# Seven block products in place of eight in the second layer, with stored sums of the weights

## The chip, the cores and the metric

The kernel runs on one core of one Trainium2 chip. The core has five engines that work side by side, each through its own instructions in order: TensorE (matrix products, PE in the profile, with PEld for the load of the operand that stays in the array), VectorE (DVE), ScalarE (ACT), GpSimd (POOL) and SyncE (SP), which here only issues DMA transfers. TensorE writes to the accumulators (PSUM), the other data live in SBUF, and DMA moves data between SBUF and the chip's memory. The metric is the device time of one execution in microseconds, the median of several runs.

## The reference, cut to what matters

The reference is an attention with a local window and block summaries, followed by two dense layers with a squared relu between them. There are 4 x 768 = 3072 tokens, 512 columns and 2048 inner columns.

```python
    k_sum = k.reshape(B, H, nb, block, D).max(axis=3)
    v_sum = v.reshape(B, H, nb, block, D).mean(axis=3)
...
    a = np.exp(scores_all)
    a = a / (np.sum(a, axis=-1, keepdims=True) + 1e-09)
    v_all = np.concatenate([v, v_sum], axis=2)
    return np.matmul(a, v_all).astype(np.float32)
...
    h = np.maximum(x @ w_in, 0.0)
    return (h * h @ w_out).astype(np.float32)
```

## The kernel before, in words

**Tiles, chunks and slots.** The 3072 tokens are 24 tiles of 128 (six for each of the four batches) and 12 chunks of two tiles (`CT` = 256 tokens). The 2048 inner columns are 16 units of 128 (`NF`). A slot does two units of one chunk, so a chunk is eight slots, numbered 0 to 7 in this document. Each operand of a product in the two layers is held as a high and a low part in a 32-bit format (float32r), and a product is made as high x high, high x low and low x high: three passes. The split weights of both layers stay in SBUF for the whole kernel, one tile `w_sb` per unit (first 512 columns for the first layer, the other 512 for the second).

**A slot** (`slot`) issues in this order: the first layer for both units (`ffn1`, L345: 2 x 12 products of 256 columns, into two accumulators `ph`), then the second layer of the slot before (`finish`, `ffn2`, L386: 2 units x 2 tiles x 3 passes = 12 products of 512 columns into `o_ps`), then for each unit the side steps of the attention that fall due and the squares (`squares`): relu on ScalarE (L354), square as the high part `gh` on ScalarE (L361), exact square on VectorE, written back over `ph` (L366), and the low part `gl` on VectorE (L370). The last step of a chunk is `evict`: ScalarE copies the two accumulators, SyncE stores them.

**The attention of later tiles** runs as twelve steps (`steps`), two per slot, one before each unit's squares (`side`) or at the slot's end (`last`). Two tiles are begun in every eight slots. From the fourth chunk on, this puts into the slots of a chunk:

- slots 0 and 4: steps 6 and 7, four transposes on VectorE (`turn`, L301) before the first unit's squares and four before the second's; for the first two tiles of a batch `place_v` stands with the second four.
- slots 1 and 5: step 8, the last four transposes before the first unit; at the slot's end `outputs` (L314) of that tile and `scores` (L238) of the next one on TensorE, with the loads of `v`, `q`, `k` and, for some tiles, the next batch's keys and values.
- slots 2 and 6: `split_x` of the finished tile and the softmax of three heads before the first unit, three more heads before the second. A head is a masked maximum on VectorE (L265) and an exponential on ScalarE (L273).
- slots 3 and 7: the inverse of the sums on VectorE (L282, L283), `norm` on POOL (L288), the last two heads and, for some tiles, `sum_k` before the first unit; the other inverse and `norm` and, for the same tiles, `sum_v` (L165, L168) before the second.

Nothing reorders this: each engine takes its instructions in the order of the program. Chunks 0 and 1 and the first seven tiles follow an order written out by hand (`START`), in which the weights are loaded and split as well.

Of the kernel before, what the change touches and what calls it, by code (L numbers as in the profile page):

```python
# [24 lines left out]
P = 128  # L25
# [5 lines left out]
NC4 = DM // P  # L31
SPARE = 1
# [38 lines left out]
def attn_ffn_kernel(ctx: ExitStack, tc: tile.TileContext, q, k, kt, v, vt, v0, w, masks, ident, mean, out):  # L71
# [6 lines left out]
    ps_s = ctx.enter_context(tc.tile_pool(name="ps_s", bufs=1, space=bass.MemoryType.PSUM))  # L78
    ps_x = ctx.enter_context(tc.tile_pool(name="ps_x", bufs=1, space=bass.MemoryType.PSUM))
    ps_h = ctx.enter_context(tc.tile_pool(name="ps_h", bufs=3, space=bass.MemoryType.PSUM))  # L80
    ps_o = ctx.enter_context(tc.tile_pool(name="ps_o", bufs=2, space=bass.MemoryType.PSUM))
# [8 lines left out]
    k_sb = [const.tile([P, 5, 2, NPAIR, NB], F32, name=f"k_sb{i}") for i in range(2)]  # L90
# [3 lines left out]
    q_sb = [const.tile([P, 2, NPAIR, 64], F32, name=f"q_sb{i}") for i in range(2)]  # L94

    e_sb = const.tile([P, H, P], F32, name="e_sb")
    pT = [const.tile([P, H, P], F32, name=f"pT{i}") for i in range(2)]
# [9 lines left out]


    def load_q(g):
        nc.sync.dma_start(out=q_sb[g % 2], in_=q[g // NT, g % NT])  # L110

    def load_k(g):
        nc.sync.dma_start(out=k_sb[g % 2][:, 0:4], in_=k[g // NT, g % NT])
# [8 lines left out]
    def sum_v0(vn):  # L122


        ps = ps_o.tile([P, DM], F32, name="o_ps")
# [44 lines left out]
    def place_k(g):  # L170
        nc.vector.tensor_copy(out=k_sb[g % 2][:, 4], in_=ksum.unsqueeze(1).to_broadcast([P, 2, NPAIR, NB]))
# [58 lines left out]
    def scores(g, p0, p1):  # L230


        if g not in s_ps:
            s_ps[g] = ps_s.tile([P, 2, NPAIR, P], F32, name="s_ps")
        for p in range(p0, p1):
            for r, s in ((0, 0), (1, 1), (0, 1), (1, 0)):
                rs, ss = slice(r * 64, r * 64 + 64), slice(s * 64, s * 64 + 64)
                nc.tensor.matmul(  # L238
                    s_ps[g][ss, r, p, 0:NK], lhsT=q_sb[g % 2][rs, s, p, :], rhs=k_sb[g % 2][rs, :, s, p, :],
# [3 lines left out]
    def scores_kt(g, p0, p1):  # L243

        if g not in s_ps:
            s_ps[g] = ps_s.tile([P, 2, NPAIR, P], F32, name="s_ps")
        for p in range(p0, p1):
            for k0, k1 in ((0, 96), (96, NK)):
                for r, s in ((0, 0), (1, 1), (0, 1), (1, 0)):
# [4 lines left out]
                        s_ps[g][ss, r, p, k0:k1], lhsT=q_sb[g % 2][rs, s, p, :], rhs=keys, start=True, stop=True  # L254
# [35 lines left out]
    def turn_pe(g, half):  # L290

        tp = ps_h.tile([P, 4, P], F32, name="ph")
# [4 lines left out]
    def turn(g, n0, n1):  # L297

        blocks = [(i, j) for i in range(4) for j in ((0, 1, 3) if i % 2 == 0 else (1, 2, 3))]
        for i, j in blocks[n0:n1]:  # L300
            nc.vector.transpose(  # L301
                out=pT[g % 2][j * 32 : j * 32 + 32, :, i * 32 : i * 32 + 32],
# [5 lines left out]
    def outputs(g):  # L308
        x_ps[g] = xp = ps_x.tile([P, NPAIR, P], F32, name="x_ps")

        for s in range(2):
            for h in range(H):
# [4 lines left out]
                    rhs=pT[g % 2][:, h, s * 64 : s * 64 + 64],  # L317
# [22 lines left out]
    def ffn1(c, f):  # L340
# [64 lines left out]

    n_g = B * NT
    n_c = n_g // TPC
    behind = []  # L410

# [239 lines left out]
```

## Time and profile before

| | us |
|---|---|
| median of three runs | 627.61 (626.56 to 628.18) |
| the profiled execution | 625.83 |
| its span, first to last instruction | 624.0 |
| PE busy in the span | 600.9 |
| DVE busy | 406.6 |
| ACT busy | 298.4 |
| POOL busy | 96.3 |

The span is the part of the profiled execution that the profile covers. Matrix products overlap in the pipeline, so the busy time and the mean of one product say less than the distance between starts: twelve products of 512 columns follow each other in 2.75 us, although each is shown as 391 ns long. In the lines of a profile, "out<-in" gives the written and the read tensors, "x" the count, and "[... <-X]" the idle time of the engine before the instruction with what ended it. A line number such as L345 is that of the kernel.

### The profile page before, as it was taken

To read this page: it belongs to the slowest core of one execution; us is meant where nothing else is said; L and a number is where in the kernel's file an instruction comes from. 1 tells how busy PE (TensorE), PEld (TensorE's weight loads), DVE (VectorE), ACT (ScalarE), POOL (GpSimd) and SP (SyncE) were. 2 spreads that over 40 slices of the span, in tenths; PEclk is the share of its full clock that TensorE was granted. 3 is DMA by queue.
4 is the path that set the end of the run, shared out by engine and by line. 5 is a ranking of instruction groups with operands and counts; after the bars stand their busy time and mean duration, and the time that the engine had idled before them with its cause. 6 is when DMAs were issued, how large, how long until landed. Compare 5 with 4: busy or idle time off the path is not lost.

```text
span 624.0 us, 13376 instructions
## 1 busy us (share of the span) xinstructions
PE 600.9 (96%) x5216; PEld 538.4 (86%) x5216; DVE 406.6 (65%) x1232; ACT 298.4 (48%) x855; POOL 96.3 (15%) x83
## 2 busy tenths in 40 slices
PE   3699999999999999999999999999999999999997
PEld 2598888988989988998988989899889989889996
DVE  4789789768766857757658668567566566563222
ACT  3788987333544353443534444434525525433322
POOL 2555762001210100101201101101101001010000
PEclk9979999999999999999999999999999999999999
DMA  9999510462032231320231321311201300000000
GB/s 308 388 339 334 203 51 18 154 199 104 26 121 68 85 119 48 106 68 35 68 112 43 119 83 71 119 47 51 75 24 46 103 1 26 35 2 1 35 0 35
DMA packets 19855, 60.38 MB, mean 97 GB/s; under 512 B 2768, under 2 KB 2896, under 8 KB 17744
## 3 DMA queue, kind: packets, MB, share of 16 engines
q1 hardware_dynamic: 19792, 59.53, 28.3%
q8 instruction: 41, 0.67, 0.5%
q14 instruction: 22, 0.18, 0.1%
HBM read 53.23 MB, written 6.29 MB: 95 GB/s over the span
## 4 chain that ended last, share of the span: by engine, by line
PE 92%; DVE 3%; DMA 2%; ACT 2%; SPq 0%; issue 0%; POOL 0%; DVEq 0%; POOLq 0%
PE ph L345 42%; PE o_ps L386 41%; PE x_ps L314 4%; PE s_ps L238 3%; DMA q_sb<-in_q 1%; DMA mask_sb<-in_masks 1%; DVE w_sb L224 1%; PE s_ps L253 1%; PE ph L294 1%; ACT e_sb L273 0%; PE o_ps L129 0%; ACT w_sb L106 0%; ACT w_raw L209 0%; SPq L152 0%; DVE sm L282 0%
## 5 line engine op out<-in xcount | busy, mean ns | idle before, releaser
L345 PE MATMUL ph<-xh,w_sb 128*128 128x256 f32 x1536 | 272.8, 280 | 0.9 <-DVE w_sb L224 0.7
L345 PEld LDWEIGHTS ph<-xh,w_sb 128*128 128x128 f32 x1536 | 238.5, 189 | 10.7 <-issue 2.9
L386 PE MATMUL o_ps<-w_sb,gh 128*128 128x512 f32 x768 | 238.0, 391 | 0.0
L345 PE MATMUL ph<-xl,w_sb 128*128 128x256 f32 x768 | 213.5, 278 | 0.2 <-DVE xl L331 0.2
L386 PEld LDWEIGHTS o_ps<-w_sb,gh 128*128 128x128 f32 x768 | 137.1, 188 | 24.9 <-issue 0.2
L386 PE MATMUL o_ps<-w_sb,gl 128*128 128x512 f32 x384 | 151.4, 394 | 0.9 <-DVE gl L370 0.9
L366 DVE TENSOR_TENSOR ph<-ph,r 128x256 f32<-128x256 f32 x192 | 82.5, 430 | 101.1 <-ACT r L354 98.6
L354 ACT ACTIVATE r<-ph 128x256 f32<-128x256 f32 x180 | 67.9, 377 | 167.0 <-PE ph L345 165.9
L345 PEld LDWEIGHTS ph<-xl,w_sb 128*128 128x128 f32 x768 | 145.1, 189 | 0.4 <-DVE xl L331 0.4
L288 POOL TENSOR_TENSOR e_sb<-e_sb,sm 128x480 f32<-128x480 f32 x43 | 43.4, 1010 | 402.7 <-DVE nmx L265 356.7
L273 ACT ACTIVATE e_sb<-e_sb,nmx 128x120 f32<-128x120 f32 x192 | 73.8, 386 | 66.3 <-DVE nmx L265 66.1
L301 DVE STREAM_TRANSPOSE pT<-e_sb 32x256 f32<-32x256 f32 x216 | 94.2, 436 | 5.2 <-POOL e_sb L288 1.8
L370 DVE TENSOR_TENSOR gl<-ph,gh 128x256 fp32r<-128x256 f32 x192 | 81.5, 424 | 24.3 <-ACT gh L361 1.8
L386 PEld LDWEIGHTS o_ps<-w_sb,gl 128*128 128x128 f32 x384 | 72.2, 188 | 15.7 <-DVE gl L370 1.3
L361 ACT ACTIVATE gh<-r 128x256 fp32r<-128x256 f32 x192 | 80.2, 418 | 10.4 <-DVE r L356 4.3
L331 DVE TENSOR_TENSOR xl<-x_ps,xh 128x512 fp32r<-128x512 f32 x24 | 16.6, 691 | 51.4 <-ACT xh L328 51.4
L265 DVE CUSTOM_DVE_ANT_0 e_sb<-s_ps,mask_sb 128x120 f32<-128x120 f32 x192 | 43.9, 274 | 4.1 <-PE ph L294 1.5
L328 ACT CAST xh<-x_ps 128x512 fp32r<-128x512 f32 x24 | 14.0, 583 | 53.0 <-PE x_ps L314 52.7
L217 POOL TENSOR_TENSOR w_raw<-w_raw 128x1024 int32<-128x1024 int32 x16 | 34.3, 2148 | 26.4 <-ACT w_raw L209 10.8
L314 PEld LDWEIGHTS x_ps<-pT,v_sb 128*64 128x64 f32 x768 | 25.3, 141 | 12.9 <-issue 12.1
L273 ACT ACTIVATION_READ_ACCUMULATOR e_sb<-e_sb,nmx 128x1 f32 x192 | 36.0, 187 | 0.0
L314 PE MATMUL x_ps<-pT,v_sb 128*64 128x64 f32 x768 | 28.6, 229 | 5.2 <-issue 4.8
(46 smaller groups left out, 293.2 us busy)
## 6 DMA issues: line engine op xcount, KB each, us to landing
w_raw<-in_w SPq DMA_DIRECT2D x16, 1024.0 KB, 13.4
v_sb<-in_v SPq DMA_DIRECT2D x24, 384.0 KB, 3.8
k_sb<-in_k SPq DMA_DIRECT2D x20, 384.0 KB, 5.4
kv<-in_kt SPq DMA_DIRECT2D x16, 384.0 KB, 5.1
q_sb<-in_q SPq DMA_DIRECT2D x24, 256.0 KB, 4.2
out<-ob SPq DMA_DIRECT2D x24, 256.0 KB, 2.0
kv<-in_vt SPq DMA_DIRECT2D x12, 384.0 KB, 5.6
vn<-in_v SPq DMA_DIRECT2D x2, 768.0 KB, 10.6
```

The source lines that it names most:

```text
L217: nc.gpsimd.tensor_tensor(out=hi, in0=hi, in1=lo, op=ALU.add)
L265: nc.vector.tensor_tensor_reduce(out=e_sb[:, h, 0:NK], in0=s_ps[g][:, h % 2, h // 2, 0:NK], in1=m, scale=-scale, scalar=3.0e38, op0=ALU.ad ...
L273: nc.scalar.activation(e, e, AF.Exp, bias=nmx[half][:, i : i + 1], scale=-1.0, accum_out=sm[half][:, i : i + 1])
L288: eng.tensor_mul(out=e, in0=e, in1=sm[half].unsqueeze(2).to_broadcast([P, 4, NK]))
L301: nc.vector.transpose(out=pT[g % 2][j * 32 : j * 32 + 32, :, i * 32 : i * 32 + 32], in_=e_sb[i * 32 : i * 32 + 32, :, j * 32 : j * 32 + 32],)
L314: nc.tensor.matmul(xp[o : o + 64, h // 2, s * 64 : s * 64 + 64], lhsT=v_sb[g % 2][:, s, h * 64 : h * 64 + 64], rhs=pT[g % 2][:, h, s * 64 ...
L345: nc.tensor.matmul(ph, lhsT=w_sb[f][:, w, cc * P : (cc + 1) * P], rhs=x[c][:, cc, :], start=(n == 0), stop=(n == 3 * NC4 - 1))
L354: nc.scalar.activation(r, ph, AF.Relu)
L361: nc.scalar.activation(gh, r, AF.Square)
L366: nc.vector.tensor_mul(out=ph, in0=ph, in1=r)
L370: nc.vector.tensor_sub(out=gl, in0=ph, in1=gh.bitcast(F32))
L386: nc.tensor.matmul(o_ps[c][tt], lhsT=g_[:, ts_], rhs=w_sb[f][:, w, DM:], start=(first and n == 0), stop=(last and n == 2),)
```

## The change

From the fifth chunk on (`WINO` = 4, counted from 0) the second layer of a slot treats its two units and two tiles as a product of 2 x 2 blocks and makes it with seven block products in place of eight (the Winograd form): `ffn2_w` issues 7 x 3 products of 256 columns into seven half banks, which sum up over the eight slots of the chunk. What the form needs besides:

- **Sums of the weights** (`w_sums`, `split_sums`): made once in chunks 2 and 3, for one pair of units in every two slots, by six POOL additions, a ScalarE copy and a POOL subtraction, and stored in the chip's memory (`t_mem`, 1 MB a pair). `load_t` fetches 1 MB back in every later slot, on POOL's queue, into one of two buffers.
- **Squares** (`squares_w`): relu, square, multiplication and low part as before, but the multiplication writes over `r` in SBUF, and high and low parts are taken for one tile less.
- **Sums of the squares** (`sums_w`): four POOL additions of 128 columns in place, at the end of a slot; then `parts_w`, in the next slot ahead of the second layer, splits the four sums with a ScalarE copy and a VectorE subtraction of 512 columns.
- **`evict_w`** at the end of a chunk: four ScalarE copies, three VectorE and four POOL additions, two stores.
- **Room**: both units of a slot share one accumulator bank, of which there are two in turn, and `outputs` takes its turn in them; all accumulators are named tiles now. From tile 6 on there is one buffer each of `q`, `k` and `pT` (`two`), so the load of the next tile's `q` and `k` is issued after `scores` of the present one. The side steps of the first unit are issued before `finish`.

```diff
+    def sums_w(k):
+        a = r_sb[:, 2 * (k % 2) : 2 * (k % 2) + 2].rearrange("p f (t c) -> p (f t) c", c=P)
+        a11, a21, a12, a22 = (a[:, i] for i in range(4))
+        add, sub = nc.gpsimd.tensor_add, nc.gpsimd.tensor_sub
+        add(out=a22, in0=a21, in1=a22)
+        sub(out=a21, in0=a11, in1=a21)
+        sub(out=a11, in0=a22, in1=a11)
+        sub(out=a12, in0=a12, in1=a11)
...
+    def squares_w(ph, k, i):
+        n = 2 * (k % 2) + i
+        r, gh, gl = r_sb[:, n], gh_sb[:, n], gl_sb[:, n]
+        cols = slice(0, P) if i == 0 else slice(0, CT)
+        nc.scalar.activation(r, ph, AF.Relu)
+        nc.scalar.activation(gh[:, cols], r[:, cols], AF.Square)
+        nc.vector.tensor_mul(out=r, in0=ph, in1=r)
+        nc.vector.tensor_sub(out=gl[:, cols], in0=r[:, cols], in1=gh[:, cols].bitcast(F32))
...
+    def parts_w(k):
...
+        s_ = r_sb[:, 2 * (k % 2) : 2 * (k % 2) + 2].rearrange("p f (t c) -> p (f t) c", c=P)
+        nc.scalar.copy(out=sh_sb[k % 2], in_=s_)
+        nc.vector.tensor_sub(out=sh_sb[2][:, k % 2], in0=s_, in1=sh_sb[k % 2].bitcast(F32))
...
+    def ffn2_w(c, k):
...
+        for p, a, b in (
+            (1, one(0, 0), raw(w0, 0)), (2, one(1, 0), raw(w1, 0)), (4, one(1, 1), tt(3)), (7, two_(1), tt(2)),
+            (5, two_(3), tt(0)), (6, two_(0), tt(1)), (3, two_(2), raw(w1, 1)),
+        ):
+            for j, (x, y) in enumerate(((a[0], b[0]), (a[0], b[1]), (a[1], b[0]))):
+                nc.tensor.matmul(
+                    acc[p], lhsT=x, rhs=y, start=(k == 0 and j == 0 and p in (1, 4, 7, 3)),
...
+    def evict_w(c):
...
+        for o, p in ((c11, 1), (c21, 4), (c22, 5), (c12, 3)):
+            nc.scalar.copy(out=o, in_=acc[p])
+        add, addp = nc.vector.tensor_add, nc.gpsimd.tensor_add
+        add(out=u2, in0=acc[6], in1=c11)
+        add(out=u3, in0=acc[7], in1=u2)
+        add(out=c11, in0=acc[2], in1=c11)
+        addp(out=u2, in0=u2, in1=c22)
+        addp(out=c21, in0=c21, in1=u3)
+        addp(out=c22, in0=c22, in1=u3)
+        addp(out=c12, in0=c12, in1=u2)
...
     def slot(c, f, side, last):
-        ph = [ffn1(c, f + i) for i in range(2)]
+        bank = next_h()
+        ph = [ffn1(c, f + i, bank[:, i * CT : (i + 1) * CT]) for i in range(2)]
+        k = f // 2
+        for do in side[0]:
+            do()
+        if behind and len(behind[0]) == 2:
+            parts_w(behind[0][1])
         done = finish()
         for i in range(2):
-            for do in side[i]:
-                do()
-            behind.append((c, f + i, *squares(ph[i]), f + i == 0, f + i == NF - 1))
-        for tt in range(TPC if done else 0):
-            evict(*done, tt, nc.scalar)
+            if i:
+                for do in side[1]:
+                    do()
+            if c >= WINO:
+                squares_w(ph[i], k, i)
+            else:
+                behind.append((c, f + i, *squares(ph[i], f + i), f + i == 0, f + i == NF - 1))
+        if c >= WINO:
+            sums_w(k)
+            behind.append((c, k))
+            if (c, k) < (n_c - 1, NF // 2 - 1):
+                load_t((k + 1) % (NF // 2))
+        if done is not None:
+            out_of_psum(done)
```

175 lines of the change are left out of this document (127 added, 48 removed).

## The prediction

> **What bounds the kernel now.** I read the page's busy times and its chain that ended last, then that chain in order of time for one stretch of 24 us, then the groups of instructions.
>
> ```profile
> span 624.0 us, 13376 instructions
> PE   600.9 (96%) x5216; PEld 538.4 (86%) x5216; DVE 406.6 (65%) x1232; ACT 298.4 (48%) x855; POOL 96.3 (15%) x83
> PE 92%; DVE 3%; DMA 2%; ACT 2%; SPq 0%; issue 0%; POOL 0%; DVEq 0%; POOLq 0%
> ```
> ```profile
> 345.52 2.92 PE ph L345 x24
> 348.44 2.75 PE o_ps L386 x12
> 351.19 2.75 PE ph L345 x24
> ...
> 362.17 2.75 PE ph L345 x24
> 364.92 2.75 PE o_ps L386 x12
> 367.67 1.08 PE x_ps L314 x32
> 368.75 0.98 PE s_ps L238 x32
> 369.73 2.92 PE ph L345 x24
> ```
>
> From 345.52 to 369.73 nothing but TensorE stands on the chain. Four slots take 24.21 us, of which the attention's products cost 1.08 + 0.98 and 0.17 at a restart. A slot without attention is 2.75 + 2.75 = 5.50 us. A product of 256 columns takes 2.75/24 = 0.1146 us, one of 512 columns 2.75/12 = 0.229: time goes by columns. So any column removed here is time, as long as what feeds TensorE keeps up. That is the question, since the change puts two more engines into that feed.
>
> **What it takes off TensorE.** The second layer of a slot goes from 12 x 512 columns to 21 x 256: 21 x 0.1146 = 2.41 us in place of 2.75, 0.34 less. A slot is then 5.16 us. With 64 slots (chunks 4 to 11): **-22.0 us**. First-layer rows (L345) already run 256 columns with a weight load each at this pace, so I add nothing for the 21 loads.
>
> **What it puts in front of TensorE.** Until now the squares of a slot go from ScalarE and VectorE straight to TensorE. Now `sums_w` (four dependent POOL additions) and `parts_w` (ScalarE copy, VectorE subtraction) stand between, and the fourth of the seven products already needs them. Prices:
>
> ```profile
> L354 ACT ACTIVATE r<-ph 128x256 f32<-128x256 f32 x180 | 67.9, 377 | 167.0 <-PE ph L345 165.9 <-DVE gl L370 1.0
> L361 ACT ACTIVATE gh<-r 128x256 fp32r<-128x256 f32 x192 | 80.2, 418 | 10.4 <-DVE r L356 4.3 <-PE o_ps L386 0.5
> L205 ACT ACTIVATE w_raw<-w_raw 128x1024 f32<-128x1024 f32 x16 | 18.5, 1154 | 1.2 <-DMA w_raw<-in_w 1.2
> L331 DVE TENSOR_TENSOR xl<-x_ps,xh 128x512 fp32r<-128x512 f32 x24 | 16.6, 691 | 51.4 <-ACT xh L328 51.4
> L641 POOL MEMSET const-float32-0.0<- 128x1 f32 x1 | 0.1, 98 | 0.2 <-issue 0.2
> ```
> ```profile
> 608.02 0.38 ACT L354 ACTIVATE r<-ph 128x256 f32<-128x256 f32 x1 [3.30 <-PE ph L345]
> 608.43 0.43 DVE L366 TENSOR_TENSOR ph<-ph,r 128x256 f32<-128x256 f32 x1 [3.14 <-ACT r L354]
> 609.00 0.42 DVE L370 TENSOR_TENSOR gl<-ph,gh 128x256 fp32r<-128x256 f32 x1
> ```
> ```profile
> L288 POOL TENSOR_TENSOR e_sb<-e_sb,sm x43: 985/987/1968, 13.9 to 548.3; 128x480 f32<-128x480 f32 x43
> ```
> ```profile
> L217 POOL TENSOR_TENSOR w_raw<-w_raw x16: 1891/1894/2957, 18.1 to 101.3; 128x1024 int32<-128x1024 int32 x16
> ```
>
> Estimates from these: a 128-column square 0.30, a 128-column VectorE subtraction 0.29, a 512-column ScalarE copy out of SBUF 0.66 (between 418 ns at 256 and 1154 at 1024), the 512-column subtraction 0.69. Hand-over between ScalarE and VectorE costs 0.03 (608.02 + 0.38 to 608.43), a VectorE step on its own result 0.14 (608.86 to 609.00). POOL at 128 columns has no row: in proportion to 987 ns at 480 it is 0.26, by the line through 1891 at 1024 it is 0.40; I take 0.335, the line from 98 ns at one column to 987. Between dependent additions I take 0.10 (ends 0 and 0.16), after VectorE 0.16. The four are 4 x 0.335 + 3 x 0.10 = 1.64.
>
> Two orders make the feed serial. First, both `ph` halves now share one bank, and work on one bank waits for the bank's other columns:
>
> ```profile
> 9.83 0.28 DVE L265 CUSTOM_DVE_ANT_0 e_sb<-s_ps,mask_sb 128x120 f32<-128x120 f32 x1 [0.42 <-DMA mask_sb<-in_masks]
> 10.22 0.59 PE L253 MATMUL s_ps<-kv,q_sb 64*64 64x96 f32 x8 [3.02 <-DVE nmx L265]
> 11.10 0.40 PE L253 MATMUL s_ps<-ksum,q_sb 64*64 64x24 f32 x8
> 11.55 0.28 DVE L265 CUSTOM_DVE_ANT_0 e_sb<-s_ps,mask_sb 128x120 f32<-128x120 f32 x1 [1.44 <-PE s_ps L253]
> ```
>
> Here pairs 2 and 3 of tile 0 wait for VectorE reading pair 1, and the read at 11.55, of pair 1 as well and written long before, waits for them. So the first relu waits for both first-layer units, and the second relu for the first multiplication. Second, the multiplication now overwrites `r`, so it waits for the square that reads `r`; the first POOL addition overwrites what the second subtraction reads, so it waits for that.
>
> Count from S, the end of the previous slot's `parts_w` subtraction, which VectorE must finish before the next multiplication (ScalarE has by then done relu and square of unit 0). Multiplication to 0.43, subtraction 0.57 to 0.85 (VectorE); relu 0.46 to 0.84, square to 1.26 (ScalarE); multiplication 1.29 to 1.72, subtraction 1.86 to 2.28; POOL 2.44 to 4.08; copy 4.11 to 4.77; subtraction 4.80 to 5.49. **The loop is 5.49 us, TensorE's slot 5.16**: even without attention the gain is gone (5.50 before). With it, by the slot's number in the chunk:
>
> ```profile
> 349.69 0.38 ACT L273 ACTIVATE e_sb<-e_sb,nmx 128x120 f32<-128x120 f32 x1
> 350.07 0.36 ACT L354 ACTIVATE r<-ph 128x256 f32<-128x256 f32 x1
> 354.09 0.16 DVE L282 TENSOR_SCALAR sm<-sm 128x4 f32<-128x4 f32 x1
> 354.29 0.18 DVE L283 RECIPROCAL sm<-sm 128x4 f32<-128x4 f32 x1
> 354.38 0.92 DVE L165 TENSOR_REDUCE vsum<-kv 128x24 f32<-128x768 f32 x1
> ...
> 355.34 0.32 DVE L168 TENSOR_SCALAR vsum<-vsum 128x24 f32<-128x24 f32 x1
> ...
> 359.54 1.78 DVE L301 STREAM_TRANSPOSE pT<-e_sb 32x256 f32<-32x256 f32 x4
> 361.36 0.43 DVE L366 TENSOR_TENSOR ph<-ph,r 128x256 f32<-128x256 f32 x1
> ```
>
> - Slots 0 and 4: four transposes (1.78) stand between the two units on VectorE: second multiplication at 0.85 + 1.78 = 2.63 in place of 1.29. Loop 6.83.
> - Slots 2 and 6: three exponentials stand between the two relus; the relu at 350.07 comes 1.38 after the first subtraction's end (348.27 + 0.42), so 2.23 in place of 0.46. Loop 7.26.
> - Slots 3 and 7: the inverse (0.16, 0.18) fits ahead of the second multiplication, 5.49; where `sum_v` comes too (0.92, and 0.32 for its scaling) 1.2 more, in five tiles (11, 14 to 17).
> - Slots 1 and 5: TensorE sets the pace. After the low parts arrive: ten products 1.15, attention 1.08 + 0.98, first layer 2.92, then relu and square 0.74: 6.87.
>
> ```profile
> 348.27 0.42 DVE L370 TENSOR_TENSOR gl<-ph,gh 128x256 fp32r<-128x256 f32 x1
> ```
>
> Sum of four: 26.45 against 24.21, **+2.24**. Thirteen such groups (chunks 4 to 9, half of 10): +29.1. The five `sum_v`: +5.9. `place_v`'s four transposes (0.305 each) in tiles 12 and 18: +2.4. At six chunk starts `evict_w`'s three VectorE additions (3 x 0.43 + 2 x 0.14 = 1.57) follow the second subtraction (3.62) and precede the next slot's four transposes and the `parts_w` subtraction: 3.62 + 1.57 + 1.78 + 0.69 = 7.66 in place of 6.83, +5.0. The rest of chunk 10, with no further scores, is 6.83 + 5.89 (6.87 less 0.98) + 2 x 5.49 = 23.70 against 4 x 5.50 + 1.08 + 0.17 = 23.25, +0.4; chunk 11, without attention, 8 x 5.49 against 8 x 5.50, -0.1. These differences already contain the -22.0.
>
> ```profile
> L177 DVE STREAM_TRANSPOSE v_sb<-vsum 32x128 f32<-32x128 f32 x12 | 3.7, 305 | 0.2
> ```
>
> End: counted from S instead of from a slot's first product, the last slot ends 0.74 + 1.15 = 1.9 later. Then `evict_w` stands open: VectorE's second addition ends 0.66 after the last product, POOL follows 0.16 later with four additions (256 columns, 0.57 by the line above) 0.10 apart, 3.4 us before the first store goes out. Now it goes out as the last product ends, the second half a microsecond on:
>
> ```profile
> 619.93 0.40 PE L386 MATMUL o_ps<-w_sb,gl 128*128 128x512 f32 x1
> 620.29 1.02 SPq L404 DMA_DIRECT2D out<-ob  x2
> ```
>
> That makes +5.3 for the end. Sum: 29.1 + 5.9 + 2.4 + 5.0 + 0.4 - 0.1 + 5.3 = **+48.0**. The profiled execution took 625.83 (span 624.0 and 1.83 around it), so 673.8; the median of the three runs, 627.61, is 1.8 above that execution, so **675.6**.
>
> **Costed at nothing.** Making the sums (POOL additions, a ScalarE copy, a POOL subtraction, a store, in chunks 2 and 3): there the old eight products run, and the squares have slack (multiplication at 361.36 + 0.43, subtraction 0.14 + 0.42 on, so done at 362.35; the second layer starts at 364.92), of which the shared bank takes up to the 1.4 of one unit's first layer. POOL does 2 x 1.05 + 4 x 0.57 + 2.0 = 6.4 us in each pair of slots (11 us) with little else to do. Uncovered, I put it at up to 4 us in all. Single `q`, `k` and `pT` buffers: the next tile's load has 24 us. The load of 1 MB per slot, on POOL's queue behind `sums_w` and ahead of the next `norm`: issued at 4.1, it is needed two slots on by the third product, some 11 us after S. Rows bound it:
>
> ```profile
> GB/s 308 388 339 334 203 51 18 154 199 104 26 121 68 85 119 48 106 68 35 68 112 43 119 83 71 119 47 51 75 24 46 103 1 26 35 2 1 35 0 35
> w_raw<-in_w SPq DMA_DIRECT2D x16, 1024.0 KB, 13.4
> out<-ob SPq DMA_DIRECT2D x24, 256.0 KB, 2.0
> ```
>
> 1 MB took 13.4 in the full queue of the start; at the 339 GB/s of the third slice it moves in 3.1, with the 2.0 of a small one 5.1. I take 5.1, as the later slices stand between 1 and 123 GB/s. POOL's time to issue: 0 to 1 us, with its queue free after the additions. The Trainium skill ("DMA: Bandwidth & Descriptors", Bandwidth) gives 6.15 us for 1 MB issued this way; by it the load would still be in time, an estimate no row here tests.
>
> POOL's 1024-word addition takes 1.89 to 2.96 us in one shape, so something holds it at times. The Trainium skill ("SBUF — State Buffer", Who interferes with whom) has a rule for that: a VectorE instruction with two SBUF inputs and a POOL instruction that reads SBUF exclude each other for a whole instruction. By it the `parts_w` subtraction of slots 2 and 6 could wait for the first `norm` (0.99): 13 x 0.99 = 13 us more, 688 by that page, an estimate. The sum above stands without it.
>
> **Rivals.** (a) The chain is shorter than I price it and TensorE stays the bound. From the end of slot 2's first layer to slot 0's low parts the chain is 0.74 + 7.26 + 5.49 + 6.83 = 20.3; TensorE's own work over that way is 3 x 5.16 + 1.26 = 16.7. If the chain loses 3.6 (POOL's four additions near 0.4 us together), the time is 625.8 - 22.0 + 5.3 = 609, median 611; from 2.2 shorter on it turns faster. For it: POOL is idle 85%. Against: 98 ns for a single column. 15%. (b) Gain and waits cancel, 625 to 632: POOL at 0.20 with no gaps. 5%. (c) The load sets the pace: at 13.4 each, issued at 4.1, products continue at 17.5 every two slots, 9 us a slot, 64 x 3.5 = 220 more, near 850. Against: the free queue. 5%. (d) My chain: 75%.
>
> **How the numbers follow.** Own bounds of (d): POOL at 0.26 and no gaps takes 0.3 + 0.3 off some 50 bound slots, 30 us: 645; at 0.40 with 0.16 adds 22, with 4 for chunks 2 and 3 some 701. The range adds (b) and the upper part of (a): 620 to 703. A change within 0.3% (1.9 us) could not be told from none. Faster 0.15, same 0.05, slower 0.80.
>
> **What would show it.** TensorE idle before the fourth product in slots 1, 3, 4, 5, 7 and 0, released by `parts_w`'s copy or subtraction, 1 to 2 us each; POOL on the chain that ended last; POOL additions near 0.33; first relus starting only when both units are done; 26 to 27 us for four slots; chunk 11 slots near 5.5. Wrong if TensorE shows no idle there, or if the wait names the load.

## The result and the profile after

| | us |
|---|---|
| kernel before, median of four runs on the same chip | 627.09 (626.45 to 628.18) |
| changed kernel, median of four runs | 742.42 (742.09 to 743.91) |
| ratio, with its 95% interval | 1.184 (1.182 to 1.187) |
| span of the profiled execution, before and after | 624.0 and 740.7 |

The change makes the kernel slower by 18%. The forecast had the sign right and the size wrong: 675.6, with 703 as its upper end. Here is the head of the page of the changed kernel, with the clock of TensorE in 40 slices:

```profile
span 740.7 us, 15128 instructions
PE 636.4 (86%) x5792; PEld 587.4 (79%) x5792; DVE 480.0 (65%) x1317; ACT 337.0 (45%) x943; POOL 334.3 (45%) x491
PEclk9789999999999989989988999998999899999997
PE 0%; POOL 0%; POOLq 0%; ACT 0%; DVE 0%; issue 0%
```

TensorE is no longer the bound (86% in place of 96%), and POOL works three and a half times as long as before. The chain that ended last cannot be used here: it breaks off after a few steps at the end, so no engine holds a share of it. The waits have to tell instead:

```profile
ACT sh L502 <- POOL r L493: 144.5, 51, 4.6
POOL r L490 <- DVE gl L483: 129.6, 51, 5.0
DVE sl L503 <- ACT sh L502: 89.2, 55, 2.9
ACT r L480 <- DVE r L482: 54.4, 51, 3.1
DVE r L482 <- ACT gh L481: 50.6, 65, 1.6
PEld o_ps L521 <- DVE sl L503: 47.2, 42, 3.1
PE o_ps L521 <- DVE sl L503: 38.0, 38, 2.9
PE o_ps L521 <- ACT sh L502: 22.1, 26, 1.3
PE o_ps L521 <- DMA t_sb<-t_mem: 7.4, 4, 4.5
```

Columns: engine, tensor and line that waited, what it waited for, us in total, times, longest. Read as a ring, it is the feed that the forecast counted: POOL waits for the second low part (L483), ScalarE's copy waits for POOL, VectorE's subtraction for the copy, TensorE for the subtraction. One turn of it, in a slot of the last chunk, where no attention is left:

```profile
707.72 0.69 DVE L503 TENSOR_TENSOR sl<-r,sh 128x512 fp32r<-128x512 f32 x1 [2.85 <-ACT sh L502]
708.34 0.42 DVE L482 TENSOR_TENSOR r<-ph,r 128x256 f32<-128x256 f32 x1
710.13 0.42 DVE L483 TENSOR_TENSOR gl<-r,gh 128x256 fp32r<-128x256 f32 x1
713.40 0.69 DVE L503 TENSOR_TENSOR sl<-r,sh 128x512 fp32r<-128x512 f32 x1 [2.85 <-ACT sh L502]
```
```profile
710.64 0.45 POOL L490 TENSOR_TENSOR r<-r 128x128 f32<-128x128 f32 x1 [2.94 <-DVE gl L483]
711.17 0.46 POOL L491 TENSOR_TENSOR r<-r 128x128 f32<-128x128 f32 x1
711.71 0.46 POOL L492 TENSOR_TENSOR r<-r 128x128 f32<-128x128 f32 x1
712.25 0.46 POOL L493 TENSOR_TENSOR r<-r 128x128 f32<-128x128 f32 x1
712.81 0.57 POOL L473 DMA_DIRECT2D t_sb<-t_mem  x1
```

From subtraction to subtraction it is 713.40 - 707.72 = 5.68 us (forecast 5.49). That is close. What is not close are the slots with attention and the starts of the chunks. The length of each slot is the distance between starts of the first layer; from the third slot of the seventh chunk on:

| interval begins in slot | 2 | 3 | 4 | 5 | 6 | 7 | 0 | 1 | (4, 2) to (10, 6) |
|---|---|---|---|---|---|---|---|---|---|
| before | 5.57 | 5.50 | 5.49 | 7.65 | 5.58 | 5.49 | 5.50 | 7.65 | 313.8 |
| after | 5.32 | 8.25 | 6.65 | 8.99 | 5.31 | 8.04 | 6.48 | 13.22 | 403.9 |

The last column runs from slot 2 of chunk 4 to slot 6 of chunk 10, thirteen groups of four slots with six chunk starts: 667.80 - 263.88 and 562.39 - 248.60. The forecast added 42.4 there (thirteen times 2.24, 5.9, 2.4 and 5.0); 90.1 came. The slot after a chunk's start takes 13.2 us, and the lines there show why. (Ahead of this stretch the changed kernel is 15.3 us behind: 8.2 at the start of the fifth chunk, 243.63 against 235.45, and 7.1 from its second slot, where TensorE waits 4.5 us for the first load of stored sums. Behind it another 11.3 are lost, 72.9 us against 61.6, where the forecast added 5.6.) Columns: start, length, engine, line:

```profile
381.60 0.74 POOL L536 TENSOR_TENSOR ob<-ob 128x256 f32<-128x256 f32 x1
382.29 0.73 POOL L537 TENSOR_TENSOR ob<-ob 128x256 f32<-128x256 f32 x1
382.97 0.72 POOL L538 TENSOR_TENSOR ob<-ob 128x256 f32<-128x256 f32 x1
383.65 0.71 POOL L539 TENSOR_TENSOR ob<-ob 128x256 f32<-128x256 f32 x1
```
```profile
381.73 3.19 DVE L503 TENSOR_TENSOR sl<-r,sh 128x512 fp32r<-128x512 f32 x1
384.85 0.41 DVE L482 TENSOR_TENSOR r<-ph,r 128x256 f32<-128x256 f32 x1
```

The subtraction that lasts 0.69 us in the last chunk lasts 3.19 here, and it ends 0.56 after the last of the four additions, so it made little or no progress while POOL added. The groups put a number on the whole:

```profile
L503 DVE TENSOR_TENSOR sl<-r,sh 128x512 fp32r<-128x512 f32 x64 | 73.2, 1144 | 89.6 <-ACT sh L502 89.2
L473 POOL DMA_DIRECT2D t_sb<-t_mem x64 | 36.9, 577 | 8.5 <-PE o_ps L521 1.9 <-POOL t_sb L468 0.3 <-issue 0.3
L493 POOL TENSOR_TENSOR r<-r 128x128 f32<-128x128 f32 x64 | 29.4, 459 | 5.0
```

A mean of 1144 ns over 64 subtractions, where the median is 693. And TensorE's clock, 1.00 through the whole middle of the kernel before, drops to a half for 3.4 or 6.8 us some fifteen times, each time during or shortly after a wait of TensorE (mean 0.943 in place of 0.991).

### The profile page after: what moved, and what is told of

The parts are those of the page before. It is cut to its first block, busy times and chain, and to the rows that moved or that the text cites. A ratio compares the mean times of both kernels' runs of the same rounds, so it can differ in the third digit from the quotient of the medians.

```text
span 740.7 us, 15128 instructions
## 1 busy us (share of the span) xinstructions
PE 636.4 (86%) x5792; PEld 587.4 (79%) x5792; DVE 480.0 (65%) x1317; ACT 337.0 (45%) x943; POOL 334.3 (45%) x491
## 5 line engine op out<-in xcount | busy, mean ns | idle before, releaser
L503 DVE TENSOR_TENSOR sl<-r,sh 128x512 fp32r<-128x512 f32 x64 | 73.2, 1144 | 89.6 <-ACT sh L502 89.2
L521 PE MATMUL o_ps<-t_sb,sh 128*128 128x256 f32 x384 | 80.3, 301 | 22.3 <-ACT sh L502 22.1
L521 PE MATMUL o_ps<-t_sb,sl 128*128 128x256 f32 x192 | 61.4, 320 | 38.5 <-DVE sl L503 38.0
L482 DVE TENSOR_TENSOR r<-ph,r 128x256 f32<-128x256 f32 x128 | 54.0, 422 | 51.1 <-ACT gh L481 50.6
L521 PEld LDWEIGHTS o_ps<-t_sb,sh 128*128 128x128 f32 x384 | 62.1, 199 | 28.5 <-ACT sh L502 28.0
L418 PE MATMUL o_ps<-w_sb,gh 128*128 128x512 f32 x256 | 81.1, 398 | 0.0
L418 PEld LDWEIGHTS o_ps<-w_sb,gh 128*128 128x128 f32 x256 | 46.0, 189 | 8.7 <-ACT w_sb L134 0.2
L521 PE MATMUL o_ps<-w_sb,gh 128*128 128x256 f32 x256 | 48.4, 282 | 4.9 <-DVE ob L535 4.9
L418 PE MATMUL o_ps<-w_sb,gl 128*128 128x512 f32 x128 | 50.7, 396 | 0.9 <-DVE gl L402 0.9
L483 DVE TENSOR_TENSOR gl<-r,gh 128x128 fp32r<-128x128 f32 (+1 forms) x128 | 47.8, 374 | 4.4
```

The lines of the kernel that those rows point to most:

```text
L418: nc.tensor.matmul(o_ps[c][tt], lhsT=g_[:, ts_], rhs=w_sb[f][:, w, DM:], start=(first and n == 0), stop=(last and n == 2),)
L482: nc.vector.tensor_mul(out=r, in0=ph, in1=r)
L483: nc.vector.tensor_sub(out=gl[:, cols], in0=r[:, cols], in1=gh[:, cols].bitcast(F32))
L503: nc.vector.tensor_sub(out=sh_sb[2][:, k % 2], in0=s_, in1=sh_sb[k % 2].bitcast(F32))
L521: nc.tensor.matmul(acc[p], lhsT=x, rhs=y, start=(k == 0 and j == 0 and p in (1, 4, 7, 3)), stop=(k == NF // 2 - 1 and j == 2 and p in (2, ...
```

## The experiments

Theory 1 is the forecast's: the serial path squares, sums, split is longer than TensorE's slot. Against it or beside it stand the load of 1 MB a slot, the restructuring of buffers and order, the collision of VectorE and POOL, and the clock. The kernel before took 626.0 to 627.1 on the chips of these runs.

### 1. Eight products, all else as changed

```diff
-WINO = 4
+WINO = 12
...
-        parts_w(NF // 2 - 1)
```

> All chunks use the eight products; the sums of the weights are still made and stored in chunks 2 and 3, the shared accumulator bank, the single q, k and pT buffers and the order of the slot stay as changed. Theory 1 (the sums of the squares make the feed longer than TensorE's slot): everything dear is gone, 627 to 637, of which up to 10 is what the making of the sums and the new buffers cost (the changed kernel is 7 to 8 us late at the end of the third chunk). Rival (the restructuring of buffers and order costs the time): 700 or more.

Measured: **639.67**, ratio 1.020 (1.017 to 1.022). That is a little above the 627 to 637 of theory 1. So 12.8 us come without any of the new arithmetic of the late chunks; the forecast had this at nothing to 4. In this kernel TensorE sets the pace throughout, so what of it still counts in the changed kernel, where TensorE waits in most slots anyway, is not shown by the number. Experiment 11 splits it.

### 2. No sums of the squares

```diff
         if c >= WINO:
-            sums_w(k)
```

> The four POOL additions of the squares in each slot are left out, so the output is not that of the reference; the split, the seven products and the loads stay. Theory 1: the loop loses 4 x 0.535 = 2.1 us, falls below TensorE's 5.16 us in most slots, the time falls by about 90 to 125 us to 615 to 650, and the granted clock returns to 1.00 as the waits go. Rival (the load of 1 MB in each slot sets the pace): 725 or more. Rival (21 products of 256 columns are not cheaper than 12 of 512): above 640 with TensorE never waiting.

Measured: **664.68** (1.057 to 1.063 times before), 78 less. Less than expected came back. The number lies above 640, but the rival that seven products are not cheaper also wanted a TensorE that never waits, and TensorE still waits 14.4 us for the subtraction here. The 78 us mix two things: without the additions the issue of the load also comes earlier on POOL, which experiments 4 and 5 show to matter. Experiment 12 separates them.

### 3. Filler products ahead of the wait

```diff
+            for _ in range(8 if p == 7 and k and k % 4 != 1 else 0):
+                nc.tensor.matmul(halves[7], lhsT=one(0, 0)[0], rhs=raw(w0, 0)[0], start=False, stop=False)
```

> Eight products of 256 columns (0.92 us), whose result nobody reads, are issued ahead of the fourth product in the slots where TensorE waits there. Theory 3 (the waits make the granted clock fall to a half for 3.4 us and more, and that costs up to 25 us): the granted clock rises to 0.98 or more and the time falls by 15 to 25 us, to 717 to 727. If the clock costs nothing, because the slowed products lie in time that is waited out anyway: 742 to 750, whatever the clock does.

Measured: **739.17**, ratio 1.179 (1.176 to 1.182); the mean clock of the span rose from 0.943 to 0.962. If all drops are to one half, a mean of 0.943 is 740.7 x 0.057 / 0.5 = 84 us of them, and 0.962 is 56 us. A third of the drops went and 3 us came back, hardly more than the noise. The expected 15 to 25 did not. That fits the other expectation, that the slowed products mostly lie in time in which TensorE would wait for the subtraction anyway; that a third of the drops costs little is what the run shows. The clock is a small term here, a consequence of the waits.

### 4. The sums of the weights loaded once

```diff
-        n, t_ = 2 * (k % 2), t_sb.pop(k)
+        n, t_ = 2 * (k % 2), t_sb[0]
...
-            if (c, k) < (n_c - 1, NF // 2 - 1):
-                load_t((k + 1) % (NF // 2))
```

> The sums of the weights are loaded once, for the first pair of units, and all later slots use that copy, so the output is not that of the reference; the 63 later loads and their issues on POOL are left out. Theory 1: 728 to 742, since TensorE waited for a load 7.4 us in all and POOL's issue of 0.58 us stands after the additions. Rival (the load sets the pace): 640 or less.

Measured: **707.28**, ratio 1.129 (1.127 to 1.131): 35 us less, far more than the 7.4 us of waits for loads and less than the rival wanted. Both misjudged it. The subtraction's mean tells where it went: 776 ns in place of 1144.

### 5. The load issued by SyncE

```diff
-        nc.gpsimd.dma_start(out=t_sb[p], in_=t_mem[p])
+        nc.sync.dma_start(out=t_sb[p].bitcast(F32), in_=t_mem[p])
```

> The load of 1 MB in each slot is issued by SyncE instead of POOL; the bytes and the buffers stay. In the changed kernel POOL's next instruction (norm, or the additions that end a chunk) starts after the issue of 0.57 us, at the same moment as the subtraction of parts_w, which then lasts 1.57 (slots 3 and 7) or 3.2 us (chunk starts) instead of 0.69. Theory (the place of the issue on POOL is what the load costs): the subtraction's mean falls from 1144 to about 780 ns and the time to 707 to 720. Rival (the moved bytes themselves cost the time): 735 to 745.

Measured: **704.75**, ratio 1.126 (1.123 to 1.130). The same bytes move, and all of the 35 us and a little more are gone. First slot 3 of a chunk in the changed kernel, POOL and then VectorE:

```profile
461.51 0.46 POOL L493 TENSOR_TENSOR r<-r 128x128 f32<-128x128 f32 x1
462.08 0.57 POOL L473 DMA_DIRECT2D t_sb<-t_mem  x1
462.67 1.00 POOL L320 TENSOR_TENSOR e_sb<-e_sb,sm 128x480 f32<-128x480 f32 x1
```
```profile
462.65 1.57 DVE L503 TENSOR_TENSOR sl<-r,sh 128x512 fp32r<-128x512 f32 x1 [0.69 <-ACT sh L502]
```

Then slot 7 of the same chunk in this experiment, POOL and VectorE:

```profile
473.31 0.45 POOL L493 TENSOR_TENSOR r<-r 128x128 f32<-128x128 f32 x1
473.73 0.99 POOL L320 TENSOR_TENSOR e_sb<-e_sb,sm 128x480 f32<-128x480 f32 x1
```
```profile
474.45 0.81 DVE L503 TENSOR_TENSOR sl<-r,sh 128x512 fp32r<-128x512 f32 x1 [2.16 <-ACT sh L502]
```

The issue of 0.57 us and ScalarE's copy of 0.62 begin together, so the issue holds POOL's next instruction back until the very moment at which the subtraction begins: `norm` and subtraction meet over their whole length. Without the issue `norm` is almost through, and the subtraction loses 0.12 in place of 0.88. At a chunk's start it is the same with the additions of `evict_w` (1.1 to 1.25 us in place of 3.2). In the span from (4, 2) to (10, 6), 373.3 are left of 403.9.

### 6. The last additions of a chunk on VectorE, a slot later

```diff
-        addp(out=u2, in0=u2, in1=c22)
...
+        def rest():
+            add(out=u2, in0=u2, in1=c22)
...
+        while later:
+            later.pop()()
```

> The four POOL additions that end a chunk go to VectorE and are issued one slot later, after the squares; nothing else changes. Theory (VectorE's subtraction and POOL's additions, both with two operands in SBUF, exclude each other): the subtraction at the six chunk starts lasts 0.69 instead of 3.2 us, the time falls by 6 x 2.5 and about 2 at the last chunk's start, to 722 to 730. Rival (the chunk start is dear because the accumulators come free late): 738 to 743.

Measured: **715.01**, ratio 1.143 (1.140 to 1.145): 27 us less, more than expected. The six starts fall from 13.1 to 15.8 us to 9.1 to 10.5, so they gain 4 to 5 each and not 2.5: the multiplications queued behind the subtraction on VectorE, and POOL's sums behind those, come earlier too. That this makes up the difference is likely, but no run separates it.

### 7. Eight products, two buffers of q, k and pT for tiles 6 and 7

```diff
-        return g % 2 if g < NT else 0
+        return g % 2 if g < 8 else 0
```

> Eight products throughout as in the first experiment, and tiles 6 and 7 keep two buffers each of q, k and pT, so that the load of tile 7 goes out before the scores of tile 6. Theory (the single buffers cost once, where the hand-written order ends: TensorE waits 6.3 us for q there): 632 to 634. Rival (the rest of the 12.8 us lies in every slot): 638 to 640.

Measured: **639.36**, ratio 1.022. (Here and in the next one the key summaries of tile 7 are not written, a copy of 192 columns.) Nothing gained; the theory is wrong. The wait of 6.3 us for `q` on which it stood is that of the very first scores, which the kernel before has as well (5.9).

### 8. Five of the seven products one slot later

```diff
+        if held:
+            ffn2_w(*held.pop(0), False)
+        held.extend(p for p in behind if len(p) == 2)
...
-        if behind and len(behind[0]) == 2:
-            parts_w(behind[0][1])
         done = finish()
...
+        if held:
+            parts_w(held[0][1])
```

> The five products that need stored sums of the weights (fourth to seventh of the seven, and the third) are made one slot later, so that parts_w of a slot stands behind the next slot's squares instead of ahead of them; the end of a chunk is spread over three slots on ScalarE and VectorE; the load is issued by SyncE; two buffers of q, k and pT until tile 7. The work is that of the changed kernel. Theory 1 (the time went to the serial path of squares, sums and split; TensorE's own work is shorter): TensorE sets the pace, 608 to 622. Rival (seven products are not cheaper on TensorE, or the loads slow them): 627 or more.

Measured: **654.72**, ratio 1.046 (1.044 to 1.048): 88 less than the changed kernel with the same arithmetic, and five of eight slots last 5.2 to 5.4 us, less than the 5.50 of the kernel before. Not all of the 88 are the path: this kernel also issues the load by SyncE and takes the last additions of a chunk off POOL, and experiment 10, which does these two things alone, stands at 703.11. So 48 us went with the serial path itself, and TensorE's gain is real. It is still not faster; TensorE waits 10.2 us for low parts of the squares (L483) and 11.9 us for the first accumulators of a chunk.

### 9. The late products first

```diff
+        late_first = bool(held) and held[0][1] != 0
+        if late_first:
+            ffn2_w(*held.pop(0), False)
```

> The eighth experiment with two edits: the five late products stand ahead of the two that use the last slot's squares, except in the third slot of a chunk (TensorE waited there 10.2 us for low parts and 11.9 us for the first accumulators of a chunk), and the block summaries of the keys are written for tile 7 as well. Theory 1: both waits go, TensorE sets the pace, 616 to 634. Rival (the waits only move to the split of the sums or to the loads): 645 to 656.

Measured: **654.26**, ratio 1.046 (1.043 to 1.048): the rival was right. The two waits went and came back at the split's subtraction (13.9 us, 23 times).

### 10. Both: load by SyncE, last additions on VectorE

```diff
-        nc.gpsimd.dma_start(out=t_sb[p], in_=t_mem[p])
+        nc.sync.dma_start(out=t_sb[p].bitcast(F32), in_=t_mem[p])
...
-        addp(out=u2, in0=u2, in1=c22)
...
+            later.pop()()
```

> The load issued by SyncE and the four last additions of a chunk on VectorE one slot later, both together. Theory (both edits take away the same collision at the chunk starts): little below the load's edit alone, 697 to 704. If their gains of 38 and 27 us were of different causes: 677.

Measured: **703.11**, ratio 1.122 (1.117 to 1.126). The gains of 38 and 27 are mostly the same gain: both take the same collision away.

### 11. Eight products, sums of the weights not made

```diff
-                if n < NF // 2:
+                if n < 0:
```

> Eight products throughout as in the first experiment, and the sums of the weights are neither made nor stored. What is left against the kernel before is the order of the slot, the shared bank of the two units and the turn that the outputs take in it. If these cost the 12.8 us of the first experiment: 636 to 640. If the making of the sums costs it: 627 to 630.

Measured: **638.02**, ratio 1.019 (1.016 to 1.021). So making the sums costs little (639.67 against 638.02; the difference of 1.7 lies within the two intervals), and the order and the banks cost 11.5. The trace of the first experiment shows two pieces: a wait of 2.5 us in the third chunk, where the outputs take a bank out of turn and the first layer then waits for the low part (L402) of the slot before; and slots of 5.58 us in the mean in place of 5.50, without a wait, the products of the first layer coming 0.118 us apart or more in five of eight slots and not 0.114 (in the kernel before, in two of eight). What slows them was not tried.

### 12. Load by SyncE and no sums of the squares

```diff
-        nc.gpsimd.dma_start(out=t_sb[p], in_=t_mem[p])
+        nc.sync.dma_start(out=t_sb[p].bitcast(F32), in_=t_mem[p])
...
-            sums_w(k)
```

> The load issued by SyncE and the four POOL additions in each slot left out, so the output is not that of the reference. Against the load's edit alone (704.75) this gives the price of the additions without the collision. Theory 1 (they lie on the serial path wherever TensorE does not pace): 64 slots less the 16 that TensorE paces, at up to 4 x 0.535 us and no more than what TensorE leaves, 40 to 55 us, so 650 to 665. Rival (they are hidden and only the collision counted): 690 or more.

Measured: **661.94**, ratio 1.057 (1.054 to 1.060). Against experiment 5 the four additions cost 42.8 us, as theory 1 has it. Against experiment 2 it is 2.7 us less, and the subtraction's mean is 730 ns in both: without the additions it matters little which engine issues the load.

### 13. One relu and one multiplication for both units

```diff
+        nc.scalar.activation(r, bank, AF.Relu)
...
+        nc.vector.tensor_mul(out=r, in0=bank, in1=r)
...
+        if c >= WINO:
+            squares_joint(bank, k)
+            sums_w(k)
         for i in range(2):
             if i:
                 for do in side[1]:
```

> Only the order of the squares changes: one relu and one multiplication over the 512 columns of both units, and the second unit's side steps of the attention behind the four additions. By the serial count the second relu no longer waits for the first multiplication, and neither transposes nor exponentials stand between the units: clean slots lose about 0.5 us, slots 4 and 0 about 1.3, slots 2 and 6 about 1.5, as far as TensorE leaves room (5.2 us a slot). Theory 1: 685 to 712, with the collisions of the load's issue still there. Rival (the bank and the side steps do not lengthen the path, only POOL's additions and the collisions do): 730 to 745.

Measured: **688.15**, ratio 1.099 (1.094 to 1.103), 54 less and within what theory 1 expected. But the collisions are not all still there. The new order also moves the moments at which POOL and VectorE meet, and the subtraction's mean falls from 1144 to 852 ns; of the seven chunk starts only two still collide:

```profile
L515 DVE TENSOR_TENSOR sl<-r,sh 128x512 fp32r<-128x512 f32 x64 | 54.6, 852 | 57.8 <-ACT sh L514 57.0
```

That is 64 x 0.292 = 19 us of subtraction less, so the order by itself is worth at most some 35 of the 54. What it does shows where nothing collides: most slots of the last chunk fall from 5.7 to 5.3 or 5.4 us. Against experiment 5, in the tenth chunk, the interval from slot 3 falls from 7.32 to 6.18 and that from slot 5 from 9.08 to 7.76, while those from slots 4 and 0 rise from 5.90 to 6.96. So the shared bank and the side steps between the units were on the path, as counted, but part of the gain is paid back.

### 14. Experiments 13, 5 and 6 together, low parts last

```diff
+            passes = list(enumerate(((a[0], b[0]), (a[0], b[1]), (a[1], b[0]))))
+            if p in (7, 5, 6, 3):
+                low.append((p, *passes.pop()))
...
+        for p, j, (x, y) in low:
...
+            squares_joint(bank, k)
+            sums_w(k)
+            if done is not None:
+                out_of_psum(done)
```

> The order of the thirteenth experiment, the load issued by SyncE, the last additions of a chunk on VectorE, and in the second layer the low parts of the four products of sums behind all other passes. Theory 1 (the serial path was the whole cause): it is now 4.9 to 5.2 us in most slots, TensorE sets the pace, 618 to 640. Rival (something else holds TensorE, such as the loads or the shared bank's turn): 655 or more.

Measured: **685.66**, ratio 1.094 (1.090 to 1.098). Theory 1 expected 618 to 640; the rival's number came. But what holds TensorE is neither the loads nor the bank's turn; it is still the subtraction (19 times, 38.7 us), by an order that this kernel made itself. POOL, VectorE and TensorE in slots 3 and 4:

```profile
439.83 0.46 POOL L505 TENSOR_TENSOR r<-r 128x128 f32<-128x128 f32 x1
440.25 0.99 POOL L320 TENSOR_TENSOR e_sb<-e_sb,sm 128x480 f32<-128x480 f32 x1
```
```profile
441.27 1.78 DVE L333 STREAM_TRANSPOSE pT<-e_sb 32x256 f32<-32x256 f32 x4 [1.40 <-POOL e_sb L320]
443.08 0.69 DVE L515 TENSOR_TENSOR sl<-r,sh 128x512 fp32r<-128x512 f32 x1
```
```profile
443.83 0.63 PE L542 MATMUL o_ps<-t_sb,sl 128*128 128x256 f32 x3 [1.52 <-DVE sl L515]
```

The second `norm` now stands on POOL behind the four additions, the transposes wait for `norm` (1.40 us), the subtraction stands behind the transposes, and TensorE behind the subtraction. Slots 4 and 0 take 7.0 us by it (13 waits, 19.7 us). The other 19.0 us are six waits at chunk starts, whose second slot takes 11.3 to 13.8 us: there the additions that end the chunk, the last four of them taken over from POOL, and transposes stand ahead of the subtraction on VectorE.

```profile
365.39 1.80 DVE L333 STREAM_TRANSPOSE pT<-e_sb 32x256 f32<-32x256 f32 x4
367.21 0.69 DVE L515 TENSOR_TENSOR sl<-r,sh 128x512 fp32r<-128x512 f32 x1
367.96 0.62 PE L542 MATMUL o_ps<-t_sb,sl 128*128 128x256 f32 x3 [2.74 <-DVE sl L515]
```

Slots 2, 3, 6 and 7 are at 5.2 to 5.4 in most chunks.

### 15. Experiment 9 with the squares of experiment 13

```diff
+            if c >= WINO and i == 0:
+                squares_joint(bank, k)
+                if held:
+                    parts_w(held[0][1])
+                sums_w(k)
```

> The ninth experiment (the five products that need sums one slot later) with one relu and one multiplication for both units, the split of the last slot's sums right behind the squares, and the second unit's side steps after them. The subtraction of the split, for which TensorE waited 13.9 us and its weight loads 20, comes 1.5 to 2 us earlier in slots with transposes or exponentials. Theory 1: 618 to 635. Rival (the wait moves on to the low parts of the squares): 645 to 655.

Measured: **646.17**, ratio 1.030 (1.028 to 1.033), between the two expectations. Six of eight slots last 5.2 to 5.3 us; slots 1 and 5 last 8.3 to 9.8, with the same `norm` behind the additions.

### 16. The second norm ahead of the squares

```diff
+        if c >= WINO and k % 4 == 3:
+            side[0] += side[1][:2]
+            del side[1][:2]
...
-        bank = next_h() if steady[0] else h_bank[1]
+        bank = o_bank[3] if g in (6, 7) else next_h() if steady[0] else h_bank[1]
```

> The fifteenth experiment with two edits: in slots 3 and 7 the second inverse and norm stand ahead of the squares, so that norm is not queued on POOL behind the four additions (TensorE waited there 13 times 0.9 us for the transposes and up to 1.0 us for the split's subtraction, both behind that norm), and the outputs of tiles 6 and 7 are written to a bank that is free in the third chunk (a wait of 2.5 us once). Theory 1: 20 to 28 us less, 618 to 627, at last level with the kernel before or faster. Rival (VectorE's twelve transposes in slots 4 and 5 fill it whatever the order): 638 to 646.

Measured: **621.43**, ratio 0.990 (0.989 to 0.992), the kernel before on the same chip 627.01. It is the only version here that is faster than the kernel before, by 1%, and the interval is clear of 1. The fifth chunk begins at 239.04 in its profile, where the other versions stand at 241.6 to 244.8 and the kernel before at 235.45, so a good part of what was lost ahead of that chunk went with the bank of the outputs. The subtraction in its profile (columns: least, median and largest ns):

```profile
L515 DVE TENSOR_TENSOR sl<-r,sh x64: 679/684/693, 250.2 to 612.4; 128x512 fp32r<-128x512 f32 x64
```
```profile
PE ph L347 <- DVE pT L333: 1.9, 5, 0.6
PE o_ps L536 <- DMA t_sb<-t_mem: 1.3, 2, 0.8
```

In the changed kernel the same row reads 691/693/3333. No subtraction collides, TensorE's waits from the fifth chunk on are 3.5 us in all, and its clock is 0.990. From (4, 2) to (10, 6) it takes 556.00 - 250.25 = 305.8 us, 8.0 less than the kernel before; in the last chunk 5.18 to 5.31 us a slot.

| interval begins in slot | 2 | 3 | 4 | 5 | 6 | 7 | 0 | 1 | (4, 2) to (10, 6) |
|---|---|---|---|---|---|---|---|---|---|
| 5: load by SyncE | 5.40 | 7.52 | 6.43 | 9.10 | 5.30 | 7.33 | 6.43 | 9.59 | 373.3 |
| 12: and no sums | 5.31 | 7.19 | 5.32 | 8.10 | 5.31 | 6.25 | 5.41 | 11.30 | 339.1 |
| 14: all, short path | 5.41 | 5.20 | 7.00 | 7.76 | 5.30 | 5.21 | 6.99 | 11.86 | 356.4 |
| 16: late products | 5.41 | 5.18 | 5.28 | 7.82 | 5.28 | 5.28 | 5.28 | 7.43 | 305.8 |

## Why the prediction was wrong

**The gain on TensorE: right, a little smaller.** 21 products take 2.47 us in an undisturbed slot (forecast 2.41), the slot 5.18 to 5.28 (forecast 5.16, before 5.50). The rival of experiments 2 and 8, that seven products are not cheaper, is out.

**The feed as the bound: right.** Experiments 8 and 16 keep the arithmetic and take the path off TensorE: against experiment 10, where the load and the last additions of a chunk are off POOL too, they save 48 and 82 us (16 with further edits). Experiments 12 and 13 confirm two of its parts, POOL's additions (43 us) and the order of relus, multiplications and side steps (at most some 35 of the 54 us). Of the signs named ahead, TensorE's waits for the copy and the subtraction are there, 1 to 3 us on average in slots 1, 3, 5 and 7 of a chunk, but next to none in slots 4 and 0; slots of the last chunk take 5.64 to 5.73 us (forecast near 5.5), and four slots 29.2 (forecast 26 to 27).

**POOL's additions: under-priced.** The forecast took 0.335 us and 0.10 between, by a line through 98 ns at one column and 987 at 480. They take 0.46 and follow each other at 0.535 (710.64 to 711.17), 2.07 us in place of 1.64. Of the other two bounds, proportion (0.26) was worse and the line through 1891 (0.40) nearer. In the last chunk the loop is still only 0.19 longer, 5.68 in place of 5.49, since hand-overs were shorter than taken (second low part 2.14 after S and not 2.28, POOL 0.09 later and not 0.16).

**The load "at nothing", and the rule left out of the sum: this is the step that failed.** The forecast wrote of POOL's issue "0 to 1 us, with its queue free after the additions", and of the exclusion of VectorE's subtraction and `norm` that "the sum above stands without it". Each alone is small: the loads land in time but for four, and in experiment 5 `norm` costs the subtraction 0.12. Together they make every `norm` of slots 3 and 7 (where the loops of slots 2 and 6 end) and, which the forecast did not think of at all, every chunk's last four additions start with the subtraction. The 13 us that were named for `norm` were about right: 13 subtractions last 0.88 us longer, 11 us. What was missing are the seven chunk starts, where the subtraction lasts 2.5 us longer each, 18 us, and what is queued behind it. Experiment 5 takes 38 us away; 34 of them lie in the slots and chunk starts with these collisions and behind them, 3 in the fifth chunk's first two slots, where TensorE's wait ahead of the first product with loaded sums is 2.3 us in place of 4.5. The Trainium skill's rule ("SBUF — State Buffer", Who interferes with whom) holds here: 0.69 us alone, 0.81 and 1.57 beside one POOL instruction, 3.19 beside four. Six chunk starts were priced at 0.83 us each on VectorE's work alone and cost 4 to 7 more than slot 5 of the same chunk.

**Restructuring at nothing: wrong by 8 us here.** So much is the changed kernel late at the start of the fifth chunk. Experiment 11 has 11.5, but some of that is the slower pace of products in later slots, which counts only where TensorE sets the pace. Of the making of the sums, for which up to 4 was kept, no cost clear of the noise was found.

**The clock: not thought of**, 3 us for a third of the drops in experiment 3, hardly more than the noise.

**What the sum leaves.** 742.4 less 675.6 is 66.8 us. Experiment 5 removes 38 of them, and 8 lie ahead of the fifth chunk. Most of the other 21 lie between (4, 2) and (10, 6), where experiment 5 still takes 17 us more than forecast: its four slots from slot 2 of the tenth chunk on, almost without collisions, last 27.62 where the forecast had 26.45, and thirteen such groups make 15. The longer additions are in that, up to 0.43 us in three slots of four; how much of it they are, and how much other places where the attention meets the path, no run separates.

**The rivals.** (c), the load as the pace, is out as stated: the loads land after 5.2 us in the median (5.1 taken), and TensorE waits 7.4 us for them in all, 4.5 of it for the very first. But the load cost more than any other single thing left out, by where it is issued. (a) and (b) needed a shorter chain; the chain came out longer.

## What to carry to other kernels

Fewer products pay only if what feeds them is not made longer than they are: here 0.3 us a slot of TensorE's time was bought with four dependent POOL additions and a split, and it turned into a gain only when those were given a whole slot more and `norm` was moved ahead of them. When an instruction is put on a queue, price not only its own time but what it moves the next instruction of that queue against: a DMA issue of 0.57 us cost most of 38 us by making POOL and VectorE meet. When two waits are close, moving one only shows the other (experiments 9, 14): look at the whole queue order, also that of the attention's `norm`, before the products are reordered.

## What the runs showed of the hardware

- A VectorE subtraction with both inputs in SBUF and POOL additions on SBUF do not run at once, and a run of POOL instructions can take every turn: from 381.60 on POOL's four additions all went ahead of the subtraction of 381.73. In experiment 5, with the same 0.13 us between the starts, the subtraction got through after one addition, and the next addition lasted 1.19 us instead of 0.73:

```profile
488.70 0.74 POOL L537 TENSOR_TENSOR ob<-ob 128x256 f32<-128x256 f32 x1
489.38 1.19 POOL L538 TENSOR_TENSOR ob<-ob 128x256 f32<-128x256 f32 x1
```
```profile
488.83 1.15 DVE L503 TENSOR_TENSOR sl<-r,sh 128x512 fp32r<-128x512 f32 x1
489.90 0.41 DVE L482 TENSOR_TENSOR r<-ph,r 128x256 f32<-128x256 f32 x1
```

  What decides between the two was not tried.
- TensorE's clock can fall to a half behind two waits of only 1.25 and 1.10 us, which end at 400.39 and 402.00 (changed kernel, columns: window, its length, busy time of PE, PEld, DVE, ACT and POOL, clock, DMA share, GB/s):

```profile
398.00:401.00 3.00, 1.65 (x12) 1.23 (x10) 1.79 (x5) 2.08 (x7) 2.63 (x6) 1.00 0.08 28
401.00:404.00 3.00, 2.00 (x13) 2.00 (x14) 2.90 (x8) 0.80 (x2) 1.35 (x2) 0.85 0.95 311
404.00:407.00 3.00, 3.00 (x18) 3.00 (x17) 2.46 (x7) 0.00 (x0) 1.86 (x5) 0.58 0.12 44
```

  The half clock comes late, when TensorE is busy again, and holds for 3.4 us: (0.15 x 3 + 0.42 x 3) / 0.5. The same two waits, 1.25 and 1.10 us, end at 338.61 and 340.22 in the same slot of the chunk before, and there the clock stays at 1.00:

```profile
339.00:342.00 3.00, 1.90 (x16) 1.78 (x16) 2.61 (x7) 0.98 (x3) 1.35 (x2) 1.00 0.91 295
342.00:345.00 3.00, 3.00 (x29) 3.00 (x28) 2.18 (x5) 0.28 (x1) 2.30 (x6) 1.00 0.16 60
```

  So the length of the waits alone does not decide; what does was not tried.
